# Down weights split by GpSimd alone, in two rooms, with its own transfers; other banks and six ScalarE reads in the down product

## The chip, the core and the metric

The kernel runs on one core of a Trainium2 chip. The time is the device time of one execution in microseconds. TensorE (PE) multiplies matrices into PSUM banks, ScalarE (ACT) and VectorE (DVE) read those banks, GpSimd (POOL) works on SBUF alone here, and SyncE (SP) issues nearly all transfers (DMAs). Each engine works through its own instructions in order, and waits for others at semaphores.

## The reference

A transformer block over 2048 positions of width 576, in float32:

```python
h  = x + attention(layernorm(x)) @ wo          # 32 query heads of 18, one shared key/value head
h2 = h + ((n @ w_gate) * (n @ w_up)) @ w_down  # n = layernorm(h), inner width 4608
```

## The kernel before

**Numbers as pairs.** Products run on float32r, which keeps fewer bits than float32. A value is therefore split into a rounded part `hi` and the rest `lo = value - hi`, and a product of two values is three matmuls: hi x hi, lo x hi, hi x lo.

**Stages.** The positions come in four blocks of 512. `keys_values` normalises all positions and makes keys and values. Then comes the query stage, the loop under `rest()` in `run` (lines 930 to 950): the attention of block 0 runs in pairs of heads (`pair`: two score matmuls on TensorE, one exponential on ScalarE; `flush`: the products with the values), and between the pairs TensorE makes the queries of all blocks (`queries`), which VectorE reads, splits, and SP stores to `q_dram`. Every pass makes two pairs, moves the query generator on by `RATE`, and takes one step of the generator `down_weights`. The loop ends at pair 220 in both kernels.

Then `flag` computes whether some score is large enough to need exact maxima, the pool `p0q` (query weights and the normalised, transposed input `XT[0]` to `XT[3]`) is given back, and new tiles take its place in SBUF. `load_wo_0` loads the output projection's weights into such new tiles (`wo_r`), GpSimd casts them and VectorE subtracts. At pair 224 `guard` branches on the flag (lines 389, 390); every engine reads the flag and branches, and goes on only from there. After the rest of block 0's attention and its projection, `ffn` runs block after block. While block b is in the feed-forward part, the attention of block b + 1 is worked in between its matmuls.

**The down weights.** The down product joins two 128-row tiles of the inner width and uses seven products of halves instead of eight (Winograd's form of Strassen's scheme). It needs, for each of 17 groups of two row tiles, seven right-hand sides: three of the four halves (of two row tiles and two column halves of 288) and four sums of halves; the 18th group is plain and needs its four halves. `down_weights` makes them once, in the query stage, as hi and lo parts, and stores them to `wd_dram`; `load_wd` fetches them for every block. In the kernel before there is one room, `wd_src` and `wd_hi` of eight halves each (the two buffers of the residual pool). For each group SP loads four halves in two DMAs (line 860). GpSimd makes the four sums (line 883), casts and subtracts three of the halves (lines 863 and 867), and casts the sums. VectorE subtracts the sums' hi part (line 867, the call at line 896). SP stores in three pieces of hi and lo each (line 871). The steps stand in the program's order between pairs, so VectorE's subtraction has a fixed place among its reads of PSUM, and SP's transfers have one among the query stores.

**The down product.** `down` (line 723) goes through `STAGES`, 14 stages of three matmuls into three banks in turn. The banks are two of the kind `f` and the one of the kind `m`. The same two `f` banks hold the gate and up projections (`pg`, `pu`) of the row tile before, which ScalarE (`g`, line 803) and VectorE (`hf`, line 807) read; the `m` bank is also used by transposes and projections that `run_aux` issues behind the product. A stage's result is added to the residual either by VectorE straight from the bank (line 748), or by ScalarE's copy to `tmp` (five buffers) and GpSimd's addition (lines 752 and 753). Nine stages take the first way, five the second.

Of the kernel before, what the change touches and what calls it, by code (L numbers as in the profile page):

```python
# [57 lines left out]
class Block:  # L58
# [583 lines left out]
    def normal(self, b):  # L642
# [80 lines left out]
    def down(self, b, pair):  # L723

        pe, dve, act, sp, pool = self.pe, self.dve, self.act, self.sp, self.nc.gpsimd
        h = self.h[b]
        W = [self.wdo.pop((b, pair, j), None) for j in range(7)]
        if pair == NC - 1:
            for s in range(NQ):
                for n in range(2):  # L730
                    y = self.ps_y(2 * s + n, f"y{b}_{pair}_{s}_{n}")
                    ms = [(self.A[:, k, 2 * i + s // 2], W[2 * i + n][:, l]) for i in range(2) for k, l in ((0, 0), (0, 1), (1, 0))]
                    for j, (m, k) in enumerate(ms):
                        pe.matmul(y[:, :HD], m[:, s % 2 * P:(s % 2 + 1) * P], k, start=(j == 0), stop=(j == 5))  # L734
                    hs = h[:, s, n * HD:(n + 1) * HD]
                    dve.tensor_tensor(hs, hs, y[:, :HD], ALU.add)
                    yield
                sp.dma_start(self.out[b * TB + s * P: b * TB + (s + 1) * P, :], h[:, s, :])
            return
        banks = [self.ps_f(f"y{b}_{pair}_0"), self.ps_f(f"y{b}_{pair}_1"), self.ps_m(f"y{b}_{pair}_2")]  # L740
        for i, (t, bank, (x, w), first, (s, n), on_dve) in enumerate(STAGES):
            y = banks[bank]
            ms = [(self.A[:, k, x], W[w][:, l]) for k, l in ((0, 0), (0, 1), (1, 0))]
            for j, (m, k) in enumerate(ms):
                pe.matmul(y[:, :HD], m[:, t * P:(t + 1) * P], k, start=(first and j == 0), stop=(j == 2), skip_group_check=True)  # L745
            hs = h[:, t + 2 * s, n * HD:(n + 1) * HD]
            if on_dve:
                dve.tensor_tensor(hs, hs, y[:, :HD], ALU.add)  # L748
            else:
                z = self.tmp[:, self.n_tmp % 5]  # L750
                self.n_tmp += 1
                act.copy(z, y[:, :HD])  # L752
                pool.tensor_tensor(hs, hs, z, ALU.add)  # L753
            yield
# [83 lines left out]
            if not self.half and len(self.pend) > keep:  # L838
                self.flush(len(self.pend) - keep)

    def steps(self, on, work=iter(())):

        while on():
            self.pair()
            self.pair()
            self.run_aux(1)
            self.flush(len(self.pend) - 1)
            next(work, None)

    def down_weights(self):  # L850


        pool, sp = self.nc.gpsimd, self.sp
        src = self.hp.tile([P, 8, HD], F32, tag="h", name="wd_src")
        hi = self.hp.tile([P, 8, HD], F32R, tag="h", name="wd_hi")

        def load(p):
            if p < NC:
                for i in range(2):
                    sp.dma_start(src[:, 2 * i:2 * i + 2], self.wd[2 * p + i].rearrange("q (a d) -> q a d", a=2))  # L860

        def high(lo, n):
            pool.tensor_copy(hi[:, lo:lo + n], src[:, lo:lo + n])

        def low(eng, lo, n):

            eng.tensor_tensor(src[:, lo:lo + n], src[:, lo:lo + n], f32(hi[:, lo:lo + n]), ALU.subtract)

        def store(p, j, lo, n):
            for k, t in enumerate((f32(hi), src)):  # L870
                sp.dma_start(self.wd_dram[p, :, j:j + n, k], t[:, lo:lo + n])

        load(0)
        yield
        yield
        for p in range(NC):
            if p == NC - 1:
                high(0, 4)
                low(pool, 0, 4)
                store(p, 0, 0, 4)  # L880
                break
            for i, (x, y) in enumerate(((1, 0), (3, 4), (3, 1), (2, 5))):
                pool.tensor_tensor(src[:, 4 + i], src[:, x], src[:, y], ALU.subtract)
                if i % 2:
                    yield
            for lo, n in ((0, 1), (2, 2)):
                high(lo, n)
                low(pool, lo, n)
            store(p, 0, 0, 1)
            store(p, 1, 2, 2)  # L890
            yield
            high(4, 4)
            load(p + 1)
            yield
            yield
            low(self.dve, 4, 4)
            store(p, 3, 4, 4)
            yield
        yield

    def run(self):
        from contextlib import ExitStack
# [11 lines left out]
        with ExitStack() as st:  # L914
            pool = lambda name, bufs, **k: st.enter_context(tc.tile_pool(name=name, bufs=bufs, **k))
# [10 lines left out]
            with tc.tile_pool(name="p0q", bufs=1) as self.p0q:  # L926
                self.wq_h = self.p0q.tile([P, 5, D], F32R, name="wq_h")
                self.wq_l = self.p0q.tile([P, 5, D], F32R, name="wq_l")
                self.XT = [self.p0q.tile([P, 9, TB], F32R, tag=f"XT{b}", name=f"XT{b}") for b in range(NB)]
                with tc.tile_pool(name="qb", bufs=2) as self.qb:  # L930
                    first = self.keys_values()
                    work = self.down_weights()

                    def rest():
                        yield from first
                        for b in range(1, NB):
                            yield from self.queries(b)
                    self.cast = self.dve.tensor_copy
                    others, live, due = rest(), True, 0.0
                    while live:  # L940
                        self.pair()
                        due += RATE
                        while due > 0 and live:
                            z = next(others, None)
                            live = z is not None
                            due -= z or 0
                        self.pair()
                        self.run_aux(1)
                        self.flush(len(self.pend) - 1)
# [13 lines left out]
            self.load_w(1)  # L963
            self.load_wd(WD_BUFS - NQ)
            self.load_x(1)
# [18 lines left out]
            self.room()  # L984
            self.load_wd(WD_BUFS)
            for b in range(NB):
# [35 lines left out]
def f32(ap):  # L1022
    return ap.bitcast(F32)
# [10 lines left out]
def drain(gen):  # L1034
    for _ in gen:
        pass
# [69 lines left out]
```

## Time and profile before

| | |
|---|---|
| median of 3 runs | 2449.7 us (2448.23 to 2451.93) |
| profiled execution | 2449.81 us, its span 2448.0 us |
| granted TensorE clock, mean | 0.985 |
| busy: PE, ACT, DVE, POOL | 96%, 57%, 47%, 25% of the span |
| pair 224 passed (the guard's branch) | 390.16 us from the start |

A row of waits names who waited, for whom, and gives the sum in microseconds, the number of times and the longest. A row of the timeline gives start, length, engine, line, operation, tiles (out<-in), shape, count, and in brackets the idle time before it and what ended that. A row of groups gives count, busy time, mean length in nanoseconds, and the idle time before with its causes. SPq is the queue of SP.

### The profile page before, as it was taken

The numbers are of one execution on the slowest core, as the hardware profiler recorded it, in microseconds if no ns is written. First come the engines' busy times: TensorE is split into PE (matmuls) and PEld (weight loads), VectorE is DVE, ScalarE is ACT, GpSimd is POOL, SyncE is SP. The second block draws the span as 40 slices with busy tenths as digits, with TensorE's granted clock in tenths as the row PEclk, the third lists the DMA queues.
The fourth block names the chain that finished last, engine by engine and source line by source line (L and its number), as shares of the span: only waits on it lengthen the run. The fifth ranks groups of instructions, "written<-read, shape, count | busy, mean of one in ns | idle before, by whom it ended". The sixth has DMA issues, their size and how long they took to land.

```text
span 2448.0 us, 46452 instructions
## 1 busy us (share of the span) xinstructions
PE 2360.1 (96%) x18425; PEld 1640.9 (67%) x18425; DVE 1161.5 (47%) x2192; ACT 1405.7 (57%) x1789; POOL 618.1 (25%) x757
## 2 busy tenths in 40 slices
PE   6989887999999999999999999999999999999999
PEld 4333333466666767776677767676667678889888
DVE  7434333444444444644444445444444466566565
ACT  4767565766666666566666665656666622222222
POOL 3444441021211222212222121212122233233332
PEclk9999898999999999999999999999999999999999
DMA  4566564333333334353333332353333344645543
GB/s 137 184 215 210 183 216 163 88 110 103 114 105 113 119 115 124 116 167 115 120 115 120 113 119 89 114 167 114 115 115 120 107 154 167 200 160 190 184 160 122
DMA packets 157768, 340.25 MB, mean 139 GB/s; under 512 B 16136, under 2 KB 48392, under 8 KB 157544
## 3 DMA queue, kind: packets, MB, share of 16 engines
q1 hardware_dynamic: 157544, 337.21, 42.8%
q8 instruction: 147, 2.41, 0.4%
q14 instruction: 77, 0.63, 0.1%
HBM read 272.63 MB, written 55.67 MB: 134 GB/s over the span
## 4 chain that ended last, share of the span: by engine, by line
PE 81%; DVE 1%; ACT 1%; DMA 1%; issue 0%; SPq 0%; POOL 0%; ACTq 0%
PE y L745 16%; PE acc L505 14%; PE pg L785 14%; PE gu L785 12%; PE pu L785 11%; PE s L500 9%; PE yo L616 3%; PE y L734 1%; PE pt L543 1%; ACT P L501 0%; PE to L136 0%; PE tx L665 0%; DMA X<-X 0%; DVE h L748 0%; DMA out_dram<-h 0%
## 5 line engine op out<-in xcount | busy, mean ns | idle before, releaser
L501 ACT ACTIVATE P<-s 128x1024 f32<-128x1024 f32 x1024 | 1030.2, 1027 | 402.5 <-PE s L500 319.0
L785 PE MATMUL pg<-X,ws 64*128 64x512 f32 x2565 | 710.5, 394 | 0.2 <-DVE h L748 0.2
L785 PE MATMUL pu<-X,ws 64*128 64x512 f32 x2565 | 708.8, 393 | 0.0
L753 POOL TENSOR_TENSOR h<-h,tmp 128x288 f32<-128x288 f32 x340 | 271.7, 808 | 975.9 <-ACT tmp L752 973.4
L505 PE MATMUL acc<-P,V 128*32 128x512 f32 x4096 | 499.1, 606 | 16.8 <-DVE os L516 15.5
L785 PEld LDWEIGHTS pg<-X,ws 64*128 64x128 f32 x2565 | 472.0, 186 | 62.2 <-issue 4.4
L785 PEld LDWEIGHTS pu<-X,ws 64*128 64x128 f32 x2565 | 471.3, 186 | 44.7 <-DVE h L748 4.3
L500 PE MATMUL s<-q,kT 56*128 56x512 f32 x2048 | 479.4, 426 | 14.4 <-DVEq L390 9.6
L745 PEld LDWEIGHTS y<-wdo,room 128*128 128x128 f32 x2856 | 387.0, 188 | 57.5 <-issue 45.8
L745 PE MATMUL y<-wdo,room 128*128 128x288 f32 x2856 | 413.1, 302 | 1.7 <-DVE h L748 1.7
L500 PEld LDWEIGHTS s<-q,kT 56*128 56x128 f32 x2048 | 227.0, 187 | 215.4 <-ACT P L501 105.7
L748 DVE TENSOR_TENSOR h<-h,y 128x288 f32<-128x288 f32 x612 | 263.7, 453 | 223.9 <-PE y L745 214.5
L752 ACT COPY tmp<-y 128x288 f32<-128x288 f32 x340 | 136.0, 400 | 363.2 <-PE y L745 361.6
L785 PE MATMUL gu<-X,ws 64*128 64x512 f32 x2646 | 309.0, 389 | 0.3
L505 PEld LDWEIGHTS acc<-P,V 128*32 128x32 f32 x4096 | 114.9, 109 | 267.5 <-issue 242.0
L87 POOL CAST ws<-wr 128x1152 fp32r<-128x1152 f32 x144 | 166.4, 1155 | 503.6 <-PE pu L785 312.0
L785 PEld LDWEIGHTS gu<-X,ws 64*128 64x128 f32 x2646 | 261.2, 184 | 40.9 <-issue 4.6
L807 DVE TENSOR_TENSOR hf<-pu,g 128x512 f32<-128x512 f32 x95 | 65.7, 692 | 359.8 <-ACT g L803 359.8
L88 DVE TENSOR_TENSOR ws<-wr,ws 128x1152 fp32r<-128x1152 f32 x144 | 195.0, 1354 | 60.6 <-POOL ws L87 60.0
L88 DVE TENSOR_TENSOR room<-S,room 128x1024 fp32r<-128x1024 f32 x68 | 83.3, 1226 | 151.4 <-ACT room L87 151.4
L803 ACT COPY g<-gu 128x512 f32<-128x512 f32 x49 | 28.9, 590 | 138.7 <-PE gu L785 138.7
L87 ACT CAST room<-hf 128x256 fp32r<-128x256 f32 (+1 forms) x144 | 73.8, 513 | 45.3 <-DVE hf L807 45.1
(160 smaller groups left out, 1608.7 us busy)
## 6 DMA issues: line engine op xcount, KB each, us to landing
wdo<-wd_dram SPq DMA_DIRECT2D x492, 288.0 KB
wr<-in_wgu_dram SPq DMA_DIRECT2D x144, 576.0 KB
q<-q_dram SPq DMA_DIRECT2D x64, 216.0 KB
wd_src<-in_wd_dram SPq DMA_DIRECT2D x36, 288.0 KB
wd_dram<-wd_hi SPq DMA_DIRECT2D x18, 576.0 KB
wd_dram<-wd_src SPq DMA_DIRECT2D x18, 576.0 KB
q_dram<-qs SPq DMA_DIRECT2D x16, 504.0 KB
X<-X SPq DMA_DIRECT2D x28, 256.0 KB
```

Source lines behind the costliest of these rows:

```text
L87: (copy or self.cast)(hi, src)
L88: self.dve.tensor_tensor(lo, src, f32(hi), ALU.subtract)
L500: self.pe.matmul(s_[:, i], self.kT[o:o + 56, t * P:(t + 1) * P], q[o:o + 56, pr], start=True, stop=True)
L501: self.act.activation(p_, s_, AF.Exp, scale=SCALE)
L505: self.pe.matmul(acc[32 * j:32 * j + 32, :], self.V[:, t, :], Ps[j // 2][:, j % 2, :], start=(t == 0), stop=(t == NT - 1), skip_group_chec ...
L616: pe.matmul(y[:, :HD], m, k, start=(i == 0), stop=(i == len(ms) - 1))
L745: pe.matmul(y[:, :HD], m[:, t * P:(t + 1) * P], k, start=(first and j == 0), stop=(j == 2), skip_group_check=True)
L748: dve.tensor_tensor(hs, hs, y[:, :HD], ALU.add)
L752: act.copy(z, y[:, :HD])
L753: pool.tensor_tensor(hs, hs, z, ALU.add)
L785: pe.matmul(ps, w[o:o + 64, wk, c], X[o:o + 64, xk, c], start=(j == 0), stop=(j == 26))
L807: dve.tensor_tensor(hf, pu, g, ALU.mult)
```

## The change

Three things change.

*Down weights.* The host puts the halves of each group in another order (second half of the first row tile first), so that the load is one DMA and the seven parts lie side by side. GpSimd does all casts and subtractions, those of the sums too, and issues all transfers itself: one load and two stores of seven parts per group. From the time at which `XT[0]` is no longer needed (group 4 on), a second room lies in its place, and the groups take the rooms by turns: with two rooms the next group's load stands behind the sums of the present group, with one it stands behind the stores. What is left of the generator is drained before `p0q` is given back.

*Order.* A constant `WO_FROM` = 208 lets pairs run before `load_wo_0`; `load_x(0)` follows at once, ahead of the pairs up to the guard.

*Down product.* The banks are taken in another order: bank 2 is the first `f`, bank 0 the second `f`, bank 1 is `m`. Stages 5 and 8 go to ScalarE and GpSimd, stage 10 to VectorE: eight and six.

```diff
-                    ms = [(self.A[:, k, 2 * i + s // 2], W[2 * i + n][:, l]) for i in range(2) for k, l in ((0, 0), (0, 1), (1, 0))]
+                    ms = [(self.A[:, k, 2 * i + s // 2], W[(1, 0, 2, 3)[2 * i + n]][:, l]) for i in range(2) for k, l in ((0, 0), (0, 1), (1, 0))]
...
-        banks = [self.ps_f(f"y{b}_{pair}_0"), self.ps_f(f"y{b}_{pair}_1"), self.ps_m(f"y{b}_{pair}_2")]
+        c, a = self.ps_f(f"y{b}_{pair}_2"), self.ps_f(f"y{b}_{pair}_0")
+        banks = [a, self.ps_m(f"y{b}_{pair}_1"), c]
...
     def down_weights(self):
-        pool, sp = self.nc.gpsimd, self.sp
-        src = self.hp.tile([P, 8, HD], F32, tag="h", name="wd_src")
-        hi = self.hp.tile([P, 8, HD], F32R, tag="h", name="wd_hi")
+        pool = self.nc.gpsimd
+        rooms = [(self.hp.tile([P, 8, HD], F32, tag="h", name="wd_src"), self.hp.tile([P, 8, HD], F32R, tag="h", name="wd_hi"))]
 
         def load(p):
             if p < NC:
-                for i in range(2):
-                    sp.dma_start(src[:, 2 * i:2 * i + 2], self.wd[2 * p + i].rearrange("q (a d) -> q a d", a=2))
...
+                if len(rooms) == 1 and self.XT[0] is None:
+                    e = self.p0q.tile([P, 9 * TB], F32R, tag="XT0", name="wd_room").rearrange("p (k j d) -> p k j d", k=2, d=HD)
+                    rooms.append((f32(e[:, 0]), e[:, 1]))
+                rooms.append(rooms.pop(0))
+                pool.dma_start(rooms[0][0][:, 0:4], self.wd[p])
+
+        def parts(room, lo, n):
+            src, hi = (t[:, lo:lo + n] for t in room)
+            pool.tensor_copy(hi, src)
+            yield
+            pool.tensor_tensor(src, src, f32(hi), ALU.subtract)
 
         load(0)
         yield
         for p in range(NC):
...
             yield
+            room = src, hi = rooms[0]
+            a, n = (1, 7) if p < NC - 1 else (0, 4)
+            if p < NC - 1:
+                for i, (x, y) in enumerate(((0, 1), (3, 4), (3, 0), (2, 5))):
+                    pool.tensor_tensor(src[:, 4 + i], src[:, x], src[:, y], ALU.subtract)
+                    if i % 2:
+                        yield
+            if len(rooms) == 2:
+                load(p + 1)
+            drain(parts(room, a, 4 - a))
             yield
+            if p < NC - 1:
+                yield from parts(room, 4, 4)
+            for k, t in enumerate((f32(hi), src)):
+                pool.dma_start(self.wd_dram[p, :, 0:n, k], t[:, a:a + n])
             yield
+            if len(rooms) == 1:
+                load(p + 1)
...
                         yield from first
+                        self.XT[0] = None
...
                         next(work, None)
+                    drain(work)
             self.flag()
             self.wp, self.hh, self.p2 = pool("w", 2), pool("hid", 4), pool("P2", 1)
+            self.steps(lambda: self.n_pair < WO_FROM)
             self.load_wo_0()
-            self.steps(lambda: self.n_pair % (2 * NT), work)
-            drain(work)
             self.load_x(0)
+            self.steps(lambda: self.n_pair % (2 * NT))
...
+WO_FROM = 208
 STAGES = [(0, 0, P1, True, (0, 0), True), (1, 1, P1, True, (0, 0), True), (0, 2, P5, True, (1, 1), False),
-          (0, 0, P6, False, (0, 1), True), (1, 1, P6, False, (0, 1), False), (0, 2, P3, False, (0, 1), True),
-          (0, 0, P7, False, (1, 1), False), (1, 1, P7, False, (1, 1), True), (1, 2, P5, True, (1, 1), True),
-          (0, 0, P4, False, (1, 0), True), (1, 1, P4, False, (1, 0), False), (1, 2, P3, False, (0, 1), False),
+          (0, 0, P6, False, (0, 1), True), (1, 1, P6, False, (0, 1), False), (0, 2, P3, False, (0, 1), False),
+          (0, 0, P7, False, (1, 1), False), (1, 1, P7, False, (1, 1), True), (1, 2, P5, True, (1, 1), False),
+          (0, 0, P4, False, (1, 0), True), (1, 1, P4, False, (1, 0), True), (1, 2, P3, False, (0, 1), False),
           (0, 0, P2, True, (0, 0), True), (1, 1, P2, True, (0, 0), True)]
...
-    wd = i["B_w_down"].reshape(NF, P, D)
+    wd = i["B_w_down"].reshape(NC, 2, P, 2, HD).transpose(0, 2, 1, 3, 4).reshape(NC, P, 4, HD)[:, :, [1, 0, 2, 3]]
```

More of the change, by code (lines that the diff above doesn't have):

```diff
@@ L839, in fill, with steps @@
                 self.flush(len(self.pend) - keep)
-    def steps(self, on, work=iter(())):
+    def steps(self, on):
         while on():
@@ L847, in steps @@
             self.flush(len(self.pend) - 1)
-            next(work, None)
     def down_weights(self):
-        pool, sp = self.nc.gpsimd, self.sp
-        src = self.hp.tile([P, 8, HD], F32, tag="h", name="wd_src")
-        hi = self.hp.tile([P, 8, HD], F32R, tag="h", name="wd_hi")
+        pool = self.nc.gpsimd
+        rooms = [(self.hp.tile([P, 8, HD], F32, tag="h", name="wd_src"), self.hp.tile([P, 8, HD], F32R, tag="h", name="wd_hi"))]
         def load(p):
             if p < NC:
-                for i in range(2):
-                    sp.dma_start(src[:, 2 * i:2 * i + 2], self.wd[2 * p + i].rearrange("q (a d) -> q a d", a=2))
@@ L862, in high @@
[L862 to L871, printed above, removed]
+                if len(rooms) == 1 and self.XT[0] is None:
+                    e = self.p0q.tile([P, 9 * TB], F32R, tag="XT0", name="wd_room").rearrange("p (k j d) -> p k j d", k=2, d=HD)
+                    rooms.append((f32(e[:, 0]), e[:, 1]))
@@ L873, in down_weights @@
+                rooms.append(rooms.pop(0))
[5 more added lines that the diff above has]
+            pool.tensor_tensor(src, src, f32(hi), ALU.subtract)
         load(0)
         yield
-        yield
         for p in range(NC):
[L877 to L890, printed above, removed]
-            yield
-            high(4, 4)
-            load(p + 1)
+            yield
+            room = src, hi = rooms[0]
[8 more added lines that the diff above has]
+            drain(parts(room, a, 4 - a))
@@ L894, in down_weights @@
             yield
+            if p < NC - 1:
+                yield from parts(room, 4, 4)
+            for k, t in enumerate((f32(hi), src)):
+                pool.dma_start(self.wd_dram[p, :, 0:n, k], t[:, a:a + n])
             yield
[L896 to L899, printed above, removed]
+            if len(rooms) == 1:
+                load(p + 1)
     def run(self):
```

## The prediction

> **What bounds the kernel now.** I read the page's parts 1 and 2, then the busy time by stage, then the waits of TensorE and of the engines that it waits for.
>
> ```profile
> span 2448.0 us, 46452 instructions
> ...
> PE 2360.1 (96%) x18425; PEld 1640.9 (67%) x18425; DVE 1161.5 (47%) x2192; ACT 1405.7 (57%) x1789; POOL 618.1 (25%) x757
> ```
>
> ```profile
> 60.00:391.00 331.00, 284.07 (x1936) 113.98 (x1935) 121.47 (x190) 219.52 (x224) 144.30 (x167) 0.92 0.62 204
> 391.00:2448.00 2057.00, 2039.74 (x16322) 1498.18 (x16320) 995.59 (x1898) 1157.32 (x1526) 451.70 (x515) 1.00 0.40 129
> ```
>
> The columns of the second fence are the stretch, its length, busy time of PE, PEld, DVE, ACT, POOL, then the granted clock, DMA share and GB/s. From 391 us on TensorE is busy 2040 of 2057 us at the full clock: 17 us are open there. From 60 to 391 us, the stage in which the first block's attention, the query projections and the down weights' parts run together, it is idle for 47 us, and the clock is 0.92. So only this stage has much to give. Its waits, cut to 50 to 480 us:
>
> ```profile
> PE acc L505 <- DVE os L516: 15.5, 4, 7.2
> PE to L136 <- DVE ob L552: 10.9, 2, 9.0
> PE s L500 <- DVEq L390: 9.6, 1, 9.6
> PE psq L337 <- DVE qs L344: 7.9, 5, 3.3
> ```
>
> ```profile
> DVE wd_src L867 <- POOL wd_hi L863: 108.5, 14, 13.0
> ```
>
> ```profile
> POOL wd_src L883 <- DMA wd_dram<-wd_src: 104.2, 11, 13.1
> ```
>
> TensorE waits for VectorE (15.5 + 10.9 + 7.9 = 34.3 us), while VectorE stands 108.5 us at one instruction, the subtraction of line 867, behind GpSimd's cast; GpSimd stands behind the stores of the one room. The remaining 9.6 us is the branch of the guard (line 390). What leads up to it:
>
> ```profile
> 374.23 0.14 DVE L385 TENSOR_SCALAR flag<-mx 1x1 int32<-1x1 f32 x1
> 382.18 5.26 DVE L88 TENSOR_TENSOR wo<-wo_r,wo 128x576 fp32r<-128x576 f32 x5 [7.81 <-POOL wo L87]
> ```
>
> ```profile
> 368.89 2.66 POOL L867 TENSOR_TENSOR wd_src<-wd_src,wd_hi 128x1152 f32<-128x1152 f32 x1
> 381.48 4.68 POOL L87 CAST wo<-wo_r 128x576 fp32r<-128x576 f32 x5 [9.94 <-DMA wo_r<-in_wo_dram]
> ```
>
> ```profile
> 371.57 0.36 SPq L871 DMA_DIRECT2D wd_dram<-wd_src  x1
> ...
> 377.20 1.31 SPq L597 DMA_DIRECT2D wo_r<-in_wo_dram  x3
> ```
>
> ```profile
> 390.16 1.22 PE L500 MATMUL s<-q,kT 56*128 56x512 f32 x4 [9.59 <-DVEq L390]
> ```
>
> The projection weights `wo_r` go where the query stage's tiles lay. Their load starts at 377.2, lands at 381.5 (4.3 us), GpSimd casts, VectorE subtracts, and TensorE passes the branch at 390.2, 8.7 us after the landing. The changed kernel keeps this chain at the same place in the program (after pair 220; `WO_FROM` = 208 is below that, so its loop runs no step), but the new room is one of those tiles: the load now also waits until GpSimd's stores from it have landed. The last of them are those of group 16 of 0 to 17. So GpSimd's chain can set the time at which everything passes the branch.
>
> **Costs in the query stage.** Taken away: 17 subtractions on VectorE, and its 108.5 us of standing; on SP 36 loads and 104 stores. VectorE's part of TensorE's waits, 34.3 us, would go, and with it some of the clock lost after each. None of it counts unless GpSimd's chain ends early enough. That chain I work out from these rows:
>
> ```profile
> L883 POOL TENSOR_TENSOR wd_src<-wd_src 128x288 f32<-128x288 f32 x68 | 55.8, 842 | 162.9 <-DMA wd_dram<-wd_src 104.2 <-DMA q_dram<-qs 28.1 <-DVE qs L344 10.5
> L867 POOL TENSOR_TENSOR wd_src<-wd_src,wd_hi 128x576 f32<-128x576 f32 x17 | 24.2, 1425 | 1.4
> L863 POOL CAST wd_hi<-wd_src 128x1152 fp32r<-128x1152 f32 x18 | 21.6, 1198 | 6.0 <-DMA wd_src<-in_wd_dram 6.0
> L867 POOL TENSOR_TENSOR wd_src<-wd_src,wd_hi 128x288 f32<-128x288 f32 x17 | 13.7, 804 | 1.4
> L863 POOL CAST wd_hi<-wd_src 128x576 fp32r<-128x576 f32 x17 | 11.3, 667 | 0.0
> L863 POOL CAST wd_hi<-wd_src 128x288 fp32r<-128x288 f32 x17 | 7.2, 426 | 0.0
> ```
>
> ```profile
> 66.30 3.20 POOL L883 TENSOR_TENSOR wd_src<-wd_src 128x288 f32<-128x288 f32 x4
> ```
>
> Work of one group: four sums, 3.2 us. Then a cast and a subtraction of 864 columns (667 + (667 - 426) = 0.91; 1425 + (1425 - 804) = 2.05) and of 1152 (1.20, and 2.66 from the row at 368.89): 6.8 us. Together 10.0 us, against 7.7 before, since VectorE's subtraction comes over.
>
> The transfers. A group stores 2 x 128 x 7 x 288 x 4 B = 2.06 MB in two DMAs of 896 rows each, and loads 0.59 MB in one.
>
> ```profile
> q1 hardware_dynamic: 157544, 337.21, 42.8%
> ```
>
> ```profile
> 311.07 0.41 SPq L871 DMA_DIRECT2D wd_dram<-wd_hi  x1
> 311.54 0.67 SPq L871 DMA_DIRECT2D wd_dram<-wd_src  x1
> ```
>
> ```profile
> 317.97 1.69 POOL L883 TENSOR_TENSOR wd_src<-wd_src 128x288 f32<-128x288 f32 x2 [9.37 <-DMA wd_dram<-wd_src]
> ```
>
> 337.21 MB in 42.8% of 2448 us are 322 GB/s: 6.4 us for the pair of stores, with nothing added. The quoted pair of 2 x 576 KB took 6.9 us from the first issue to its release, of which 3.7 at that rate; the 3.2 on top are start, landing and other traffic ahead on SP's queue. So a pair takes 6.4 to 9.6 us; I take 8.3, nearer the upper end, as start and landing stay. The load I take at the 4.3 us of `wo_r`.
>
> What GpSimd pays to issue a DMA no row shows. The nearest are SP's issue of such a store, and GpSimd's smallest instruction:
>
> ```profile
> L871 SPq DMA_DIRECT2D wd_dram<-wd_hi x52: 332/371/997, 75.6 to 368.8; - x52
> ```
>
> ```profile
> L1094 POOL MEMSET const-bfloat16-1.0<- 128x1 bf16 x1 | 0.1, 102 | 0.0
> ```
>
> Lower end 0.37 us, SP's median. Upper end for a store, if GpSimd spends 0.1 us on each of the 56 rows that fall to one of 16 DMA engines: 5.6 us. I take 1.0 us for each of the three, SP's longest: an issue is nearest to an issue.
>
> The Trainium skill ("DMA: Bandwidth & Descriptors", section "Anatomy of one DMA — SWDGE (gpsimd) path") gives 2.0 us plus the bytes at 436 GB/s for one of GpSimd's DMAs. An estimate by it, the two stores taken as one, has the pair in 6.7 us and the load in 3.4; the sum below would then be 2431 instead of 2461. No run so far shows such a DMA here. Against the change speaks "SBUF — State Buffer", section "SBUF: two separate sides": while VectorE runs a copy in its two-port mode, GpSimd cannot write descriptors; no run here shows that either.
>
> **The sum.** GpSimd is free for the first load at 66.3; landed at 66.3 + 1.0 + 4.3 = 71.6. With one room nothing overlaps: 10.0 work + 2.0 issues + 7.3 until the second store has landed (8.3 less the 1.0 between the two) + 1.0 + 4.3 = 24.6 a group. Group 3 is ready at 71.6 + 3 x 24.6 = 145.4, its stores issued at 157.4. From group 4 on there is a second room: its load, 5.3 us later, at 162.7; sums until 165.9; load of group 5 until 166.9; 6.8 + 2.0 gives 175.7. With two rooms the load still stands in the queue between the sums and the casts, and waits for the previous group's second store; everything behind it on GpSimd waits too. A group then takes 7.3 + 1.0 + 6.8 + 2.0 = 17.1 us, the 3.2 us of sums being inside the 7.3. Group 16: 175.7 + 12 x 17.1 = 380.9; landed 388.2; `wo_r` + 4.3, branch + 8.7: 401.2. Before, it was 390.2: **11 us later**. TensorE gets there some 35 us earlier, and stands.
>
> Group 17's stores run beside the load of `wo_r`, and the loads of `h` wait for them behind it; both are needed only 12 pairs later and cost nothing. SP's queue has no store of weights any more; nothing waited for it at the end.
>
> **The down product.** Bank 0 now takes the up projection's buffer, so stage 0 waits for `hf`.
>
> ```profile
> 506.83 0.69 DVE L807 TENSOR_TENSOR hf<-pu,g 128x512 f32<-128x512 f32 x1 [3.02 <-ACT g L803]
> ```
>
> ```profile
> 509.65 6.04 PE L745 MATMUL y<-wdo,room 128*128 128x288 f32 x42
> 515.62 0.50 PE L500 MATMUL s<-q,kT 56*128 56x512 f32 x2
> ```
>
> `hf` is done 2.1 us ahead of the first matmul, so that wait costs nothing; without this cover it would be one stage, 6.04 / 14 = 0.43 us, in 68 products, 29 us. A read moved to ScalarE (400 ns against VectorE's 453) and GpSimd (808 ns) has slack:
>
> ```profile
> L752 ACT COPY tmp<-y 128x288 f32<-128x288 f32 x340 | 136.0, 400 | 363.2 <-PE y L745 361.6
> L753 POOL TENSOR_TENSOR h<-h,tmp 128x288 f32<-128x288 f32 x340 | 271.7, 808 | 975.9 <-ACT tmp L752 973.4
> ```
>
> The shared bank is now free only after the last stage, which can cost a transpose right behind it half a microsecond; a handful of those, against 1.9 us that line 616 lost. I set it at 0, bounds -2 and +4. The plain product's new order of weights follows the host's order, at no cost.
>
> So: 2448.0 us of span lie in an execution of 2449.8 (the runs' median is 2449.7), and 2449.8 + 11.0 = **2461 us**.
>
> **Rivals.** *Cheap transfers (faster).* Each 0.1 us of issue price moves the sum by some 3.6 us. At SP's 0.37 and a pair of 8.3 a group takes 15.8 us and the branch comes at 378.6: 2438; with a pair of 7.4, 2424; at both lower ends 13.9 us, 2408. The point is 0.7 us an issue at 8.3: below it the kernel is faster. For it speaks that the stores leave SP's queue, where loads and query stores stood ahead of them; against it, that it needs an issue at the hardware queue's price. The Trainium skill's page on DMA, by the estimate above, comes out on this side.
>
> *Dear descriptors.* At 3 us a store the group takes 19.1 us and the sum is 2497, at 5.6 us 22.0 and 2546: GpSimd's issuing is then the bound.
>
> *GpSimd hidden.* Should its chain end before TensorE gets to pair 220, the branch comes 34 us or more earlier: 2415, or 2400 with the clock kept. It would need a group in under 14 us, when 10.0 are plain work. The change would then do what its relief of VectorE allows.
>
> *The product.* A wait for `hf` in every product, 2479 to 2490. The 2.1 us speak against it.
>
> **How the numbers follow.** The forecast, GpSimd's chain with moderate prices, 2446 to 2490: 0.46, with 0.09 of it within 0.2% (5 us, about what a measurement here can tell from no change). Cheap transfers 0.30, dear descriptors 0.16, hidden 0.06, the product 0.02. Faster 0.36, same 0.09, slower 0.55. The range reaches from 2410, near the cheap end, to 2540, near the dear one; the forecast's own is 2446 to 2490.
>
> **What would show it.** Right: TensorE's waits for `os`, `ob` and `qs` gone, one long wait at line 390; VectorE waiting for GpSimd's `wo`; groups some 17 us apart with GpSimd idle ahead of the load; the branch at about 401. Wrong: groups 14 or 16 us apart, or GpSimd's issues of several microseconds; a wait at line 745.

## The result, and the profile after

The changed kernel took 2468.2 us (median; 2457.73 to 2470.32) against 2449.5 for the kernel before: ratio 1.0067, 95% interval 1.0037 to 1.0096. The execution that the profile shows is the shortest of these, 2457.73 us, with a span of 2455.9. Measured again later, beside the experiments, it took 2456.58 us (ratio 1.0038, 1.0021 to 1.0054). Of the twelve executions of both measurements eight took 2455.6 to 2458.7 us and four 2467.8 to 2471.1, these at a granted clock of 0.976 or 0.977 instead of 0.978 to 0.980, and no trace shows what the four lost. By the two ratios the changed kernel is slower by 0.4 to 0.7%; the forecast of 2461 us stands between the two medians. How the number came about differs from the forecast, and that is what the rest is about.

The page of the changed kernel, span, busy times and TensorE's busy tenths:

```profile
span 2455.9 us, 46162 instructions
...
PE 2323.8 (95%) x18425; PEld 1624.4 (66%) x18425; DVE 1127.0 (46%) x2107; ACT 1431.0 (58%) x1857; POOL 749.3 (31%) x862
...
PE   5999952999999999999999999999999999999999
```

A slice is 61.4 us. In the sixth and seventh, from 307 to 430 us, TensorE is busy for only some 50 and 20% of the time, where it had some 80 and 70 before. The waits of TensorE between 50 and 480 us, after:

```profile
PE s L500 <- DVEq L390: 74.9, 1, 74.9
PE acc L505 <- DVE os L516: 5.0, 3, 2.9
PE to L136 <- DVE ob L552: 4.6, 1, 4.6
```

The waits for `os`, `ob` and `qs`, 34.3 us before, have shrunk to 9.6; `qs` is gone. In their place stands one wait of 74.9 us at the branch. The timeline leading up to it, after (engines mixed, in order of time):

```profile
335.51 0.14 DVE L385 TENSOR_SCALAR flag<-mx 1x1 int32<-1x1 f32 x1
...
383.06 0.57 POOL L862 DMA_DIRECT2D wd_src<-in_wd_dram  x1 [3.39 <-DMA wd_dram<-wd_src]
...
390.34 1.84 POOL L889 DMA_DIRECT2D wd_dram<-wd_room  x2
...
398.84 1.65 SPq L597 DMA_DIRECT2D wo_r<-in_wo_dram  x2
...
404.70 4.67 POOL L87 CAST wo<-wo_r 128x576 fp32r<-128x576 f32 x5 [7.16 <-issue]
...
405.40 5.25 DVE L88 TENSOR_TENSOR wo<-wo_r,wo 128x576 fp32r<-128x576 f32 x5 [69.75 <-POOL wo L87]
...
415.59 1.31 PE L500 MATMUL s<-q,kT 56*128 56x512 f32 x4 [74.93 <-DVEq L390]
```

The flag is there at 335.6, but GpSimd issues group 16's stores out of the new room only at 390 to 392. The load of `wo_r` follows 7 us later, GpSimd's cast 6 us after that, and VectorE's subtraction stands behind the cast. What the load of `wo_r` (line 597) waits for is in the waits of SP's queue, between 50 and 480 us:

```profile
SPq L597 <- DMA wd_room<-in_wd_dram: 36.9, 1, 36.9
...
SPq L597 <- DMA wd_dram<-wd_room: 26.9, 1, 26.9
```

It waits for the new room, first for the last load into it and then for the last stores out of it. TensorE passes at 415.6, 25.4 us later than before. The span grew by only 7.9. Somewhere behind the branch 17.5 us came back.

### The profile page after: what moved, and what is told of

The parts are those of the page before. It is cut to its first block, busy times and chain, and to the rows that moved or that the text cites. A ratio compares the mean times of both kernels' runs of the same rounds, so it can differ in the third digit from the quotient of the medians.

```text
span 2455.9 us, 46162 instructions
## 1 busy us (share of the span) xinstructions
PE 2323.8 (95%) x18425; PEld 1624.4 (66%) x18425; DVE 1127.0 (46%) x2107; ACT 1431.0 (58%) x1857; POOL 749.3 (31%) x862
## 4 chain that ended last, share of the span: by engine, by line
PE 80%; DVE 1%; ACT 1%; DMA 1%; issue 0%; SPq 0%; ACTq 0%
PE pg L786 16%; PE y L746 16%; PE acc L505 14%; PE gu L786 12%; PE s L500 9%; PE pu L786 8%; PE yo L616 2%; PE y L734 1%; PE pt L543 1%; PE to L136 0%; ACT P L501 0%; PE tx L665 0%; DVE h L749 0%; DMA X<-X 0%; DMA out_dram<-h 0%
## 5 line engine op out<-in xcount | busy, mean ns | idle before, releaser
L754 POOL TENSOR_TENSOR h<-h,tmp 128x288 f32<-128x288 f32 x408 | 318.7, 811 | 919.9 <-ACT tmp L753 918.7
L500 PE MATMUL s<-q,kT 56*128 56x512 f32 x2048 | 438.5, 424 | 79.7 <-DVEq L390 74.9
L505 PE MATMUL acc<-P,V 128*32 128x512 f32 x4096 | 493.4, 601 | 5.7 <-DVE os L516 5.0
L746 PE MATMUL y<-wdo,room 128*128 128x288 f32 x2856 | 403.7, 300 | 1.3 <-DVE h L749 1.2
L500 PEld LDWEIGHTS s<-q,kT 56*128 56x128 f32 x2048 | 194.8, 186 | 276.8 <-issue 135.8
L753 ACT COPY tmp<-y 128x288 f32<-128x288 f32 x408 | 162.6, 399 | 327.5 <-PE y L746 320.7
L749 DVE TENSOR_TENSOR h<-h,y 128x288 f32<-128x288 f32 x544 | 235.2, 454 | 243.3 <-PE y L746 240.4
```

Source lines behind the costliest of these rows:

```text
L500: self.pe.matmul(s_[:, i], self.kT[o:o + 56, t * P:(t + 1) * P], q[o:o + 56, pr], start=True, stop=True)
L505: self.pe.matmul(acc[32 * j:32 * j + 32, :], self.V[:, t, :], Ps[j // 2][:, j % 2, :], start=(t == 0), stop=(t == NT - 1), skip_group_chec ...
```

## The experiments

One subtraction orders all of them: the span less the time at which TensorE passes the branch (the start of its first matmul behind it, of line 500). All kernels of this table branch after pair 224.

| kernel | median us | branch at | span less branch |
|---|---|---|---|
| before | 2449.5 | 390.16 | 2057.8 |
| down weights alone | 2477.9 | 417.99 | 2059.3 |
| banks alone | 2440.6 | 389.26 | 2048.2 |
| reads alone | 2440.2 | 389.79 | 2047.5 |
| product (banks and reads) | 2428.7 | 387.45 | 2038.8 |
| after | 2456.6 | 415.59 | 2040.3 |
| after, load later | 2420.1 | 376.93 | 2039.8 |
| after, loads on SP | 2412.4 | 371.09 | 2039.9 |
| after, all transfers on SP | 2395.9 | 353.04 | 2040.5 |

(Branch and span are of the profiled execution; for "after" they are those of its first one.) Behind the branch a kernel takes 2058 to 2059 us with the old product, 2039 to 2040 with the new one, and some 2048 with one half of its edits. Ahead of the branch the four kernels with the old down weights lie within 2.7 us of each other, so there the down weights decide.

### The two parts apart

The product's two edits in the kernel before:

```diff
-        banks = [self.ps_f(f"y{b}_{pair}_0"), self.ps_f(f"y{b}_{pair}_1"), self.ps_m(f"y{b}_{pair}_2")]
+        c, a = self.ps_f(f"y{b}_{pair}_2"), self.ps_f(f"y{b}_{pair}_0")
+        banks = [a, self.ps_m(f"y{b}_{pair}_1"), c]
...
-          (0, 0, P6, False, (0, 1), True), (1, 1, P6, False, (0, 1), False), (0, 2, P3, False, (0, 1), True),
-          (0, 0, P7, False, (1, 1), False), (1, 1, P7, False, (1, 1), True), (1, 2, P5, True, (1, 1), True),
-          (0, 0, P4, False, (1, 0), True), (1, 1, P4, False, (1, 0), False), (1, 2, P3, False, (0, 1), False),
+          (0, 0, P6, False, (0, 1), True), (1, 1, P6, False, (0, 1), False), (0, 2, P3, False, (0, 1), False),
+          (0, 0, P7, False, (1, 1), False), (1, 1, P7, False, (1, 1), True), (1, 2, P5, True, (1, 1), False),
+          (0, 0, P4, False, (1, 0), True), (1, 1, P4, False, (1, 0), True), (1, 2, P3, False, (0, 1), False),
```

> The kernel before with the down product's two edits alone (the order of its banks, the three reads that leave VectorE and the one that comes to it). Theory now: the product is what gained, 17.7 us by the offset between the two traces, so about 2432 us (2428 to 2437), with each of 68 products at 5.91 us where the first 46 or so no longer push the gate and up products out of step. The forecast's step (the product at 0, bounds -2 and +4): 2447.5 to 2453.5. Rival: the offset shrank because the branch had come late (work that was held back is caught up), and the product is worth nothing: 2450.

Measured: 2428.72 us (ratio 0.9917, 0.9901 to 0.9934), 20.8 us below the kernel before. The forecast's step is refuted, and so is the rival in which late work is caught up: here nothing was late.

The changed kernel with the old `banks` and `STAGES` (it keeps the change of order too, which was not run by itself):

> The changed kernel with the down product as it was before, so the down weights' part of the change alone. Theory now: the branch comes at about 415 us as in the changed kernel, 25 us later than before, and nothing makes up for it: 2475 us (2470 to 2487, the upper part if the runs of the changed kernel that were 10 us above its profiled one are the rule). The forecast's sum (branch 11 us later, product 0): 2461. Rival (what was held back is caught up later): about 2458.

Measured: 2477.91 us (1.0116, 1.0099 to 1.0133), 28.4 us above. The branch of this kernel, and its first down product (before: 509.65, a row that the prediction shows):

```profile
417.99 1.32 PE L500 MATMUL s<-q,kT 56*128 56x512 f32 x4 [71.75 <-DVEq L390]
...
536.89 6.05 PE L745 MATMUL y<-wdo,room 128*128 128x288 f32 x42
```

It is 27.8 us late at the branch, 27.2 at the first product, 29.3 at the end: a delay at the branch is carried to the end in full. The two parts add up: 28.4 - 20.8 = +7.6, or 2457.1 us, where the changed kernel measured 2456.6.

### The product's two edits apart

The order of the banks alone, in the kernel before:

> The kernel before with the order of the banks alone. Theory: after a product the first matmuls of gate and up start together again, since the up projection's buffer is free one stage earlier; that is some 0.2 us in each of 46 products, 8 us: 2441 us (2437 to 2445). The gap of a tenth of a microsecond at stages 11 and 12 stays, so products stay near 6.05 us. Rival: banks are worth nothing alone: 2450.

The three changed reads alone:

> The kernel before with the changed reads alone (stages 5 and 8 to ScalarE, stage 10 to VectorE). Theory: the third bank no longer waits for VectorE's queue, products take 5.91 instead of 6.05 us, 68 x 0.14 = 9.5 us: 2440 us (2436 to 2444), while gate and up stay out of step after each product. Rival: 2450, and the gap was made by the banks.

Measured: banks 2440.64 us (0.9965, 0.9951 to 0.9979), reads 2440.22 us (0.9964, 0.9952 to 0.9977); 8.9 and 9.3 us, together 18.2 of the 20.8. Behind the branch the two add up, by the table 9.6 and 10.3 against 19.1; the rest is ahead of it, where no down product runs. Groups by line, of TensorE: before, then reads alone, then banks alone.

```profile
L500 PE MATMUL s<-q,kT 56*128 56x512 f32 x2048 | 479.4, 426 | 14.4 <-DVEq L390 9.6 <-ACT P L501 2.5 <-DMA q<-m_dram 1.5
L745 PE MATMUL y<-wdo,room 128*128 128x288 f32 x2856 | 413.1, 302 | 1.7 <-DVE h L748 1.7
```

```profile
L500 PE MATMUL s<-q,kT 56*128 56x512 f32 x2048 | 478.9, 426 | 14.2 <-DVEq L390 9.5 <-ACT P L501 2.5 <-DMA q<-m_dram 1.5
L745 PE MATMUL y<-wdo,room 128*128 128x288 f32 x2856 | 402.6, 299 | 1.3 <-DVE h L748 1.2
```

```profile
L500 PE MATMUL s<-q,kT 56*128 56x512 f32 x2048 | 442.1, 426 | 14.4 <-DVEq L390 9.4 <-ACT P L501 2.8 <-DMA q<-m_dram 1.5
L746 PE MATMUL y<-wdo,room 128*128 128x288 f32 x2856 | 413.1, 302 | 1.8 <-DVE h L749 1.7
```

The reads take 10.5 us of busy time from the down product's rows (413.1 to 402.6) and leave the score matmuls alone. The banks leave the product at 413.1 and take busy time from the score matmuls (479.4 to 442.1), which run between the gate and up matmuls. The idle columns hardly move in either. The mean of a score matmul stays at 426 ns; busy time counts matmuls that run side by side once (2048 times 426 ns are 872 us), so the 37 us by which it falls say that the order has changed, and not what that is worth (8.9 us). What the banks do is seen behind the first product. The timeline of TensorE before, right after it:

```profile
515.96 0.43 PE L785 MATMUL pg<-X,ws 64*128 64x512 f32 x1
516.24 0.50 PE L785 MATMUL pu<-X,ws 64*128 64x512 f32 x1
516.24 0.50 PE L785 MATMUL pg<-X,ws 64*128 64x512 f32 x1
```

and of the kernel with the banks alone:

```profile
514.27 0.40 PE L786 MATMUL pu<-X,ws 64*128 64x512 f32 x1
514.27 0.62 PE L786 MATMUL pg<-X,ws 64*128 64x512 f32 x2
514.51 0.38 PE L786 MATMUL pu<-X,ws 64*128 64x512 f32 x1
514.74 0.39 PE L786 MATMUL pg<-X,ws 64*128 64x512 f32 x1
```

`pg` and `pu` use 64 rows of TensorE's array each. With the new order the first two start together at 514.27, and the next pair follows every 0.23 us. Before, `pu` starts 0.28 us behind `pg`, beside the second `pg`, and the pairs run out of step. Its buffer was bank 1, which the product's last stage used, so it waited for VectorE's last read; the new order ends on bank 0 and the `m` bank, and `pu` gets its buffer one stage earlier. TensorE worked on `pg` meanwhile, so the rows of its matmuls show no wait. The rows of its weight loads (PEld) do, before and with the banks alone:

```profile
L785 PEld LDWEIGHTS pu<-X,ws 64*128 64x128 f32 x2565 | 471.3, 186 | 44.7 <-DVE h L748 4.3
```

```profile
L786 PEld LDWEIGHTS pu<-X,ws 64*128 64x128 f32 x2565 | 472.2, 186 | 23.7
```

The weights of `pu` waited for VectorE's read of the product (`h`, line 748), 4.3 us in all, and this wait is gone. `pg` and `pu` come next behind 44 of the 68 products. Counted from their starts, `pu` came 0.2 to 0.3 us behind `pg` in 33 of the 44 before, in 33 with the reads alone and in one with the banks alone. An estimate from that, 33 times 0.28 us or 9.2, is near the 8.9 measured. Which of the three reads gave the 9.3 us was not tried apart. That it is the third bank's (stage 8, which stage 11 must wait for) is argued from the starts in the trace: before, the matmuls 33 and 34 of a product (counted from 0, the first two of stage 11) started 188 and 238 ns behind their forerunners (median of 68 products), most others some 132; with the reads alone these gaps are gone. Over 68 products they come to 11 us, an estimate near the 9.3 measured.

### Is the wait GpSimd's chain?

The changed kernel beside three others, on one chip:

> The changed kernel as it is, beside the next three on one chip. Its first profiled execution took 2457.7 us and its three other runs 2468 to 2470. The two parts alone gave 2477.9 (weights) and 2428.7 (product) against 2449.5, so the sum of both is 2457.1 us. Theory: the two parts add up, 2455 to 2460. Rival: together they cost some 10 us more than apart, 2466 to 2470.

Measured: 2456.58 us, where the parts give 2457.1. The parts add up. The next edit moves the branch behind 32 more pairs:

```diff
-WO_FROM = 208
+WO_FROM = 240
```

> The changed kernel with WO_FROM at 240 instead of 208: the projection weights are loaded after pair 240 and the branch stands after pair 256 instead of 224. GpSimd's chain stays as it is. Theory: the branch still comes at about 415 us, since GpSimd's stores out of the new room set it, but TensorE has 32 more pairs to do until then, some 36 us of the 75 that it stood: about 2424 us (2418 to 2438). Rival (the wait is not behind GpSimd's chain but in the load and splitting of the projection weights behind whatever comes before them): the branch moves later by as much as TensorE worked, and the time stays at 2455 to 2460.

Measured: 2437.98 us (0.9946, 0.993 to 0.9963). The branch:

```profile
411.88 1.31 PE L500 MATMUL s<-q,kT 56*128 56x512 f32 x4 [35.36 <-DVEq L390]
```

It comes at 411.9, nearly as before the edit, though 32 more pairs are done by then, and the wait fell from 74.9 to 35.4 us. So GpSimd's chain sets the time of the branch, as said. But the gain is 18.6 us and not 36: behind the branch this kernel saves only 14 us for 32 pairs fewer (2438.3 - 411.9 = 2026.4 against 2040.3). 32 pairs filled 39.5 us of the wait, 1.2 us each, and behind the branch, where pairs run between the gate and up matmuls, leaving them out freed 0.4 us each. Why a pair costs so much less there was not tried.

The load of the next group behind three quarters of the group's work:

```diff
-            if len(rooms) == 2:
-                load(p + 1)
             drain(parts(room, a, 4 - a))
             yield
             if p < NC - 1:
-                yield from parts(room, 4, 4)
+                last = parts(room, 4, 4)
+                next(last)
+                yield
+            if len(rooms) == 2:
+                load(p + 1)
+            if p < NC - 1:
+                drain(last)
```

> The changed kernel with the load of the next group, in the part with two rooms, moved from behind the sums to ahead of the last subtraction, so that GpSimd does 4 us more of a group's work before it stands for the stores of the group before. Theory: the standing at that load (43 us at two-room groups) is most of what the chain has over its work; a group takes 13.5 to 14.5 instead of 17.7 us, the stores of group 16 are issued at 340 to 352 instead of 392, the branch passes at 365 to 376 instead of 415: 2408 to 2420 us. Rival: the transfers themselves are the bound (2.65 MB a group, load and stores sharing one queue), the wait moves to the next group's sums, which wait for the later load: a group stays above 16.5 us, 2440 to 2458.

Measured: 2420.14 us (0.9884, 0.9865 to 0.9904), at the upper end of the theory's range. The waits of GpSimd ahead of that load between 50 and 400 us, after and with the load later:

```profile
POOL wd_src L862 <- DMA wd_dram<-wd_src: 49.6, 9, 8.7
POOL wd_room L862 <- DMA wd_dram<-wd_room: 34.4, 6, 8.1
```

```profile
POOL wd_src L862 <- DMA wd_dram<-wd_src: 31.9, 5, 8.8
...
POOL wd_room L862 <- DMA wd_dram<-wd_room: 7.4, 5, 3.0
```

84.0 us of standing become 39.3. A group with two rooms takes 14.4 us instead of 17.8 (group 4's stores to group 16's, over 12), and the branch comes at 376.9, a microsecond behind the theory's 365 to 376.

Both edits:

> The last two together. Theory: GpSimd's chain ends before 352 us and TensorE gets to pair 256 at about 377, so nothing stands at the branch and all of the 75 us goes: 2383 to 2395 us. Rival (transfers are the bound, a group above 16.5 us): like the run with the branch after pair 256 alone, 2418 to 2438.

Measured: 2411.85 us (0.9835, 0.9815 to 0.9854), a miss by 17 us. The wait at the branch is 8.8 us, so little is left to gain from GpSimd there; but the early pairs are again worth less than they cost (2410.4 - 387.2 = 2023.2), and GpSimd's chain ended at 363 instead of 351, since groups 3 and 4, around the start of the second room, took 31 and 26 us in this run. Why was not tried.

### Who issues the transfers

```diff
-                pool.dma_start(rooms[0][0][:, 0:4], self.wd[p])
+                self.sp.dma_start(rooms[0][0][:, 0:4], self.wd[p])
...
-                pool.dma_start(self.wd_dram[p, :, 0:n, k], t[:, a:a + n])
+                self.sp.dma_start(self.wd_dram[p, :, 0:n, k], t[:, a:a + n])
```

> The changed kernel with the down weights' loads and stores issued on SP again, everything else as changed: SP stands for the stores' landing ahead of the next load, and GpSimd goes on. Theory (the branch is late because GpSimd itself stands 84 us for landings and spends some 2.2 us a group on issues): a group takes 13 to 15 us as in the run with the later load, the projection weights are loaded at 345 to 360 and the branch passes at 362 to 378; against that the query stores stand on SP behind those waits, and TensorE's waits for qs come back (7.9 us before). 2412 to 2430. Rival (it is the transfers' own time that sets a group, by whatever queue): a group stays at 17 us or more and the time at 2445 to 2465. Rival (SP's standing holds up the query stage as in the kernel before): above 2440 with over 30 us of TensorE's waits behind VectorE.

Measured: 2395.94 us (0.9778, 0.9762 to 0.9794), better than the theory's range, and 60.6 us below the changed kernel. Both rivals fall. A two-room group takes 13.2 us, a one-room group 21.8 (24.5 in the changed kernel). The waits of TensorE, and its branch:

```profile
PE s L500 <- DMA q<-q_dram: 8.4, 1, 8.4
PE psq L337 <- DVE qs L344: 6.0, 1, 6.0
PE acc L505 <- DVE os L516: 4.9, 2, 2.9
```

```profile
353.04 1.32 PE L500 MATMUL s<-q,kT 56*128 56x512 f32 x4 [8.44 <-DMA q<-q_dram]
```

SP's standing holds the query stores up a little: `qs` is back with 6.0 us, no more. So one part of the change, that GpSimd issues the transfers, is enough to account for the loss: without it the change is 53 us faster than the kernel before. TensorE's 8.4 us are taken up below. To see what of that is the load and what the stores, the first of the two edits alone:

> The changed kernel with the down weights' loads alone issued on SP; the stores stay on GpSimd. With both on SP the time fell to 2396. GpSimd's price has two parts: its standing ahead of the load until the stores of the other room have landed (84 us in all), which goes with the load, and its issue of two stores, some 1.6 us a group, which stays. Theory (the standing is the cost): a group takes 13 to 15 us, the projection weights are loaded by 345 to 362, and the time is 2395 to 2412. Rival (stores through GpSimd's queue land later than through SP's, and that sets the group): a group at 16 us or more and 2425 to 2450.

Measured: 2412.39 us (0.9841, 0.9819 to 0.9863), at the theory's edge. Of the 60.6 us, 44 go with the loads, where GpSimd stood for the landing of stores, and 16.5 with the stores. A two-room group takes 14.2 us. Two reasons for the stores' part can be seen, and were not tried apart. GpSimd no longer spends 1.5 us a group on issuing two stores. And the order differs. On GpSimd both stores stand behind the last subtraction. On SP the `hi` store can start as soon as its cast is done. The timeline of SP with both on SP, one of the groups that had one room:

```profile
100.68 0.52 SPq L889 DMA_DIRECT2D wd_dram<-wd_hi  x1
103.71 0.52 SPq L889 DMA_DIRECT2D wd_dram<-wd_src  x1
```

3.0 us apart, against 0.8 on GpSimd. From 250 us on most pairs on SP are under 2 us apart, so the order can act in the first half above all.

### Is it the projection weights that hold up the branch?

On the kernel with the later load, the weights' load and split go behind the branch (`WO_FROM` = 244):

```diff
-            self.steps(lambda: self.n_pair < WO_FROM)
-            self.load_wo_0()
-            self.load_x(0)
             self.steps(lambda: self.n_pair % (2 * NT))
             self.flush(len(self.pend))
             self.guard()
-            self.wo_from = self.n_pair + 12
+            self.steps(lambda: self.n_pair < WO_FROM)
+            self.load_wo_0()
+            self.load_x(0)
+            self.wo_from = self.n_pair + 12
```

> The kernel with the later load, and the projection weights' load and split moved behind the branch: the branch stands after pair 224 as in the changed kernel, the load after pair 244 (WO_FROM). Theory: what TensorE waits for at line 390 is not the guard's flag but the split of the projection weights that stands ahead of the branch on VectorE; with it behind, the 29 us at the branch go to under 3, pairs 224 to 256 run while GpSimd's chain ends, and the projection finds its weights ready: 2395 to 2406 us, below both the run with the later load (2420) and the one with both changes (2412). Rival (VectorE standing at the split holds up os, so the wait comes back at acc or at the projection, line 616): 2409 to 2422.

Measured: 2399.35 us (0.9804, 0.9783 to 0.9824). The time is as the theory has it, the wait is not: 29.3 us became 8.1, not under 3. The instructions of line 390 in this kernel (count, then shortest, median and longest in ns, and when), and TensorE's matmul behind it:

```profile
L390 PEldq COMPARE_BRANCH  x1: 5512/5512/5512, 337.3 to 337.3; - x1
L390 DVEq COMPARE_BRANCH  x1: 72/72/72, 338.6 to 338.6; - x1
...
L390 DVEq EVENT_SEMAPHORE  x1: 21/21/21, 344.9 to 344.9; - x1
```

```profile
345.17 1.31 PE L500 MATMUL s<-q,kT 56*128 56x512 f32 x4 [8.07 <-DVEq L390]
```

What is left is the branch itself: TensorE's branch takes 5.5 us, and VectorE, for which the first matmul waits, comes back 6.3 us after its own (338.6 to 344.9). What either spends this time on no view shows. In the kernel before, TensorE's branch took 7.1 us (380.1 to 387.2), so most of the 9.6 us for which the prediction shows the chain of the projection weights would by that have been there without it.

Both together, the transfers on SP and the weights behind the branch:

> The transfers on SP and the projection weights behind the branch (load after pair 244, branch after pair 224) together. In the run with the transfers on SP, TensorE still stood 8.4 us at its first matmul behind the branch, at 353 us, which the trace puts down to the load of q; VectorE had finished the projection weights' split at 350.5. Theory (it is again the split ahead of the branch): the 8.4 us go and the time is 2386 to 2392. Rival (it is the load of q, late behind the waits on SP): the wait stays and the time is 2394 to 2400.

Measured: 2405.32 us (0.9816, 0.98 to 0.9833): slower than with SP alone, and outside both ranges. The wait stays, 7.4 us. VectorE's return from the branch, and TensorE's first matmul:

```profile
L390 DVEq EVENT_SEMAPHORE  x1: 21/21/21, 356.5 to 356.5; - x1
```

```profile
356.76 1.32 PE L500 MATMUL s<-q,kT 56*128 56x512 f32 x4 [7.36 <-DMA h<-in_x_dram]
```

The trace puts the wait down to a load of `h`. But TensorE takes the branch in 5.7 us, VectorE is back after 6.4 and 0.3 us ahead of that matmul, as in the run before; so it is read here as the branch, which is argued and not shown. The same holds for the 8.4 us with the transfers on SP: TensorE's branch took 6.4 us there, and VectorE was back at 352.7, 0.3 us ahead of the matmul at 353.04. And with the projection allowed only from pair 256 on, the feed-forward part starts with 16 more pairs done (the matmuls of line 500 ahead of it: 594 against 562) but 22 us later, and gets back only part. The best median found is that of the changed kernel with its transfers on SP, 2395.9 us; the run with the weights behind the branch, 2393.0 to 2406.7, cannot be told from it.

## Why the prediction was right, and where not

**The waits of the query stage: right.** 34.3 us of TensorE's waits for VectorE became 9.6, TensorE was at the branch at 340.7 instead of 380.6, 40 us earlier (forecast 35), and stood there; the relief of VectorE bought nothing. From 60 us until TensorE got to the branch, before and after (the columns are those of the prediction's second fence):

```profile
60.00:381.00 321.00, 283.23 (x1932) 113.46 (x1931) 115.61 (x184) 219.52 (x224) 139.62 (x162) 0.92 0.62 203
```

```profile
60.00:341.00 281.00, 269.52 (x1932) 109.52 (x1931) 112.79 (x167) 218.52 (x224) 181.05 (x160) 0.97 0.58 189
```

For the same 1932 matmuls TensorE was idle 11.5 us instead of 37.8, and busy 13.7 us less at a granted clock of 0.97 instead of 0.92: the prediction's "some of the clock lost" is a third of the 40.

**GpSimd's chain: right in kind, too short.** Forecast +11 us at the branch, measured +25.4 (27.8 with the weights alone). Work of a group: 10.0 forecast, 10.1 in the rows of group 16 (3.5 for the sums, then 0.9, 2.0, 1.1 and 2.6). Issue prices, by the instruction's durations after:

```profile
L889 POOL DMA_DIRECT2D wd_dram<-wd_src x11: 759/1050/1069, 82.3 to 396.8; - x11
...
L862 POOL DMA_DIRECT2D wd_src<-in_wd_dram x11: 555/572/772, 66.4 to 383.1; - x11
```

A load takes 0.57 us, the second store of a pair starts 0.8 behind the first, and both take 1.5: 2.1 us a group where the forecast had 3.0. The "dear descriptors" rival, 3 us a store and more, falls (at its upper end a group is 22.2 us by its own terms, not 22.0). One-room groups took 24.5 us (24.6). Two-room groups took 17.8 (17.1), between 15.6 and 20.9. The mis-sized term is the landing: from the end of the two issues to the next load 8.8 us on average instead of 7.3, which eats more than the 0.9 that the issues saved. It varies more than a single 8.3 a pair says, 4.2 to 12.5 us for one store.

The 14.4 us missing at the branch are +3.0 until group 4, +8.0 over twelve groups, -0.3 at the last landing, and +3.7 behind it: 1.6 in the load of `wo_r`, beside which group 17's stores ran (the forecast set that at nothing; with the transfers on SP they were issued 10 us ahead of it or more, and it took 4.2 us again), and 2.2 from GpSimd's cast to the passing of the branch, 10.9 for 8.7, nearly all of it in VectorE's branch (5.0 us for 3.1).

The "cheap transfers" rival begins at 0.7 us an issue with a pair of 8.3 us. The issues came to just that, 0.7 us on average, but the landings were longer, so it falls. The Trainium skill's page "DMA: Bandwidth & Descriptors", section "Anatomy of one DMA — SWDGE (gpsimd) path", gives 3.4 us for the load and 6.7 for the pair, an estimate by its formula of 2.0 us plus bytes at 436 GB/s. Measured was 4.2 for the load (median; up to 10.2) and 6.9 for a single store of the pair (median), and 10.3 on average from the first store's issue to the next load in a group with two rooms. By the formula the time would have been the 2431 of the prediction, and it was not. Of the Trainium skill's page "SBUF — State Buffer", section "SBUF: two separate sides", by which VectorE's copies in a two-port mode keep GpSimd from writing descriptors, there is no sign: no issue took longer than 1.1 us. In which mode VectorE's copies ran the trace does not say, so this is no test of it.

**The down product: wrong, and this is the step that failed.** "I set it at 0, bounds -2 and +4"; it is -20.8 us by itself. What it had looked at held: no matmul of the product waits for `hf`, and a transpose waits five times, 2.7 us in all. What failed is the reading above it, that from 391 us on "17 us are open there". TensorE was busy 2040 of 2057 us, but busy rows held the loss: stages spaced wider inside a product, and gate and up matmuls out of step. The matmuls' rows of waits show neither; the starts of successive matmuls show both, and the weight loads' waits the second.

**The sum.** 2461 forecast, 2457.1 from the parts: +28.4 where +11 stood, -20.8 where 0 stood. Direction and size came out because two errors of 17 and 21 us cancelled, which is luck; only the first number's mechanism was in the forecast.

## What to carry to other kernels

Two kernels with the same work can be compared from a fixed point, here the branch: span less branch told at once which part of the change acted where. A full TensorE is no proof that nothing is to be had from its order; compare the starts of successive matmuls, above all where half-array products should run in pairs, and look at the waits of the weight loads too. A transfer put on the queue of a computing engine makes that engine stand for whatever the transfer waits for; place it where its wait has run out, or leave it on a queue that does nothing else.

## What was not expected of the hardware

- Two 64-row matmuls in step took 0.23 us a pair. Behind 33 of 44 products the second started some 0.28 us behind the first, with no wait in the matmuls' rows; the order of banks that ended this was worth 8.9 us over the kernel.
- The branch on a loaded value at line 390 took TensorE 5.5 us with the weights behind it (3.7 and 7.1 in the changed kernel and the kernel before), with VectorE back 6.3 us after its own; 8.1 us of standing remained with the projection weights out of its way.
- GpSimd's issue of a store of 896 rows took 0.76 to 1.08 us, SP's 0.5; both are short beside the landing, and what cost was the standing.
